# SwiGLU feed-forward: the early loads in one queue, and the first tokens in two pieces

## The chip, the cores and the metric

The kernel runs on one core of a Trainium2 chip. The metric is the device time of one execution in microseconds. All positions below are microseconds from the start of the profiled span. TensorE is written PE, VectorE DVE, ScalarE ACT, GpSimd POOL and SyncE SP; SPq and ACTq are the rows of the DMA issues of SP and ACT, and PEld the weight loads of PE.

## The reference

```python
B, S, D, F = 1, 2048, 512, 1376      # bf16: x (B, S, D), w_gate, w_up (D, F), w_down (F, D)

def reference(x, w_gate, w_up, w_down):
    g = silu(x @ w_gate)
    u = x @ w_up
    return (g * u) @ w_down
```

## The kernel before

The 2048 tokens are four chunks of 512. F is cut into ten whole tiles of 128 and a rest of 96. For each chunk and tile, PE makes a gate product (kind G) and an up product (kind U) of 128 F rows by 512 tokens in one PSUM bank each: four steps over D (`dk`), each of two matmuls of 64 columns that stand side by side in the array. ACT puts Silu of G into `sg_sb`, DVE multiplies it with U into `hT_sb`. The rest of 96 is handled by the kinds X and Y. At the end PE multiplies `hT_sb` with `w_down` (kind O), ACT and DVE copy the banks to `o_sb`, and SP (once ACT) stores them.

The products need the tokens transposed, D on the partitions, in `xT_sb`. For chunks 1 to 3 and for tokens 256 to 511 a transposing DMA does this (`load_x`; the load of tokens 256 to 511 is called `x0b`). Tokens 0 to 255 come in by a plain load into `xn_sb` (name `xn`), with two neighbouring tokens on each partition: partition p holds tokens 2p and 2p + 1. PE transposes them with an identity, in four groups of kind T: for piece i = 0, 1 and half h = 0, 1 of D, four transposes into a bank. DVE copies the half 0 to `xT_sb` and ACT the half 1 (`xt_ready[i, h]`). Since the columns of `xT_sb` are then every second token, the first two stores write every second row (`rows_of`).

The order on each engine is written out by hand:

- ACT first issues the load of the gates of F tiles 0 and 1 (`wg0`, `loads_on_scalar`), then does a dummy Silu that brings in its table, then its work in the order of the groups.
- SP issues `xn`, then the ups of F tiles 0 and 1 (`wu0`), then `x0b`, then the slabs of F tiles 2 to 3, 4 to 6 and 7 to 10 (gates, ups), the last ups, `x1` to `x3`, and the parts of `w_down`. All are issued without a wait. The stores come behind.
- POOL makes the index tile from which DVE makes the identity.
- PE runs `N_WARM` = 6 matmuls of ones, 512 columns wide, and `N_FILL` = 2 of 128 columns, into a bank that is not yet used. Then it waits for the identity and for `xn`, and runs the 16 transposes. Then the products of F tiles 0 and 1 of chunk 0 in parts: G of tile 0 for tokens 0 to 127 and 128 to 255, then G of tile 1, U of tile 0, U of tile 1 for tokens 0 to 255, then the same four for tokens 256 to 511. From there each product is whole. `need(name)` is a wait of PE for a load, made once for each load; `after` is a wait for a copy or another step of ACT or DVE.

A load's semaphore is named after it (`s_xn`, `s_wg0`, `s_wu0`, `s_x0b`). PE counts its finished groups in `s_P`.

Of the kernel before, what the change touches and what calls it, by code (L numbers as in the profile page):

```python
# [6 lines left out]
BF16 = mybir.dt.bfloat16  # L7
FP32 = mybir.dt.float32

N_WARM = 6  # L10
N_FILL = 2


def bass_standalone__swiglu_ffn__prompt_kernel(nc, x, w_gate, w_up, w_down, out):
    _, S, D = x.shape
    F = w_gate.shape[1]
    P = 128
# [12 lines left out]
    HT = SC // 2  # L30
    HC = P // 2
    NXN = HT // P
# [5 lines left out]
    xf = x[0]  # L38
    of = out[0]
# [7 lines left out]
    with ExitStack() as es:  # L47
# [20 lines left out]
        xn_sb = sb("xn_sb", [P, NXN, D], BF16)  # L68
# [12 lines left out]
        def load_sem(name):  # L81
            loads[name] = sem(f"s_{name}")
            return loads[name]
# [6 lines left out]
        def load_x(eng, name, t0, t1):  # L90
            eng.dma_start_transpose(
                xT_sb[:, :, t0:t1], xf[t0:t1, :]
            ).then_inc(load_sem(name), 16)

        def load_w(eng, name, src, base, f0, f1):
            eng.dma_start(
                w_sb[:, :, base + f0:base + f1],
                src[:, f0:f1].rearrange("(k p) f -> p k f", p=P),
            ).then_inc(load_sem(name), 16)

        slabs = [(0, 2), (2, 4), (4, 7), (7, NFT)]
        slab_of = {ft: a for a, b in slabs for ft in range(a, b)}

        def load_slab(eng, a, b):
            load_w(eng, f"wg{a}", w_gate, 0, a * P, min(b * P, F))
            load_w(eng, f"wu{a}", w_up, UPH, a * P, min(b * P, F - 32))

        def loads_on_scalar(act):
            load_w(act, "wg0", w_gate, 0, 0, slabs[0][1] * P)

        def loads_on_sync(sp):
            sp.dma_start(
                xn_sb[:, :, :].rearrange("p j d -> p (j d)"), xf[0:HT, :].rearrange("(p j) d -> p (j d)", j=NXN)
            ).then_inc(load_sem("xn"), 16)
            load_w(sp, "wu0", w_up, UPH, 0, slabs[0][1] * P)
            load_x(sp, "x0b", HT, SC)
            for a, b in slabs[1:]:
                load_slab(sp, a, b)
            load_w(sp, "wut", w_up, F - (F - 32), F - 32, F)
            for c in range(1, NSC):  # L120
                load_x(sp, f"x{c}", c * SC, (c + 1) * SC)
            sp.dma_start(
                wd_sb[:, 0:NFF, :], w_down[0:NFF * P, :].rearrange("(k p) d -> p k d", p=P)
            ).then_inc(load_sem("wd"), 16)
            for c in range(NSC):
                sp.dma_start(
                    wdt_sb[R * c:R * (c + 1), :, :], w_down[NFF * P:F, :].rearrange("(q p) d -> p q d", p=R)
                ).then_inc(load_sem(f"wdt{c}"), 16)
            sp.dma_start(wdl_sb[:, :], w_down[NFF * P:F, LASTA:D]).then_inc(load_sem("wdl"), 16)
# [7 lines left out]
        def add_group(kind, **what):  # L137
            g = dict(kind=kind, at=len(groups), bank=banks[len(groups) % NB], readers=[], **what)
            groups.append(g)
            return g  # L140
# [9 lines left out]
        def tview(bank):  # L150
            return bank[:, 0:P].bitcast(BF16).rearrange("p (k t) -> p k t", k=2)
# [60 lines left out]
        for i in range(NXN):  # L212
            for h, eng in enumerate("DA"):
                g = add_group("T", i=i, h=h)
                op = add_op(
                    eng, g, kind="copy", out=xT_sb[:, 2 * h:2 * h + 2, i * P:(i + 1) * P],
# [15 lines left out]
        for at in range(NST):  # L232
            j, c = divmod(at, NSC)
            t = c * TPC + j
            ob = at % NOS
            end = at == NST - 1
            for c0, c1 in [(0, LASTA), (LASTA, LASTB), (LASTB, D)] if end else [(0, D)]:
                g = add_group("O", t=t, c0=c0, c1=c1, c=c)
# [3 lines left out]
                    eng, g, kind="copy", out=o_sb[ob][:, c0:c1], src=g["bank"][:, 0:c1 - c0],  # L242
# [4 lines left out]
            n_store[ob] += 2 if end else 1  # L247

        def rows_of(t):
            if t < NXN:  # L250
                return of[0:HT, :].rearrange("(p j) d -> j p d", j=NXN)[t]
            return of[t * P:(t + 1) * P, :]

        def on_sync(sp):
            loads_on_sync(sp)
            for t, c0, c1, ob, eng, n in stores:
                if (c0, c1) == (0, LASTA):
                    continue
                sp.wait_ge(s_A if eng == "A" else s_D, n)
                sp.dma_start(rows_of(t)[:, c0:c1], o_sb[ob][:, c0:c1]).then_inc(s_out[ob], 16)  # L260
            for i in range(NST, NST + NOS):
                sp.wait_ge(s_out[i % NOS], 16 * n_store[i % NOS])
# [4 lines left out]
            ).then_inc(s_I, 1)  # L267

        def on_scalar(act):
            loads_on_scalar(act)  # L270
            act.activation(adummy[:, 0:4], zero_c, ACT.Silu)
            for op in act_ops:
                act.wait_ge(s_P, op["g"]["at"] + 1)
                if op["kind"] == "silu":
                    if op["free"]:
                        act.wait_ge(s_D, op["free"])
                    fn = ACT.Silu
                else:
                    if op["stored"][1]:
                        act.wait_ge(*op["stored"])  # L280
                    fn = ACT.Copy
                act.activation(op["out"], op["src"], fn).then_inc(s_A, 1)  # L282
            for t, c0, c1, ob, eng, n in stores:
                if (c0, c1) == (0, LASTA):
                    act.wait_ge(s_A, n)
                    act.dma_start(rows_of(t)[:, c0:c1], o_sb[ob][:, c0:c1]).then_inc(s_out[ob], 16)
# [16 lines left out]
        def on_tensor(pe):  # L303
            landed = set()

            def need(name):
                if name not in landed:
                    pe.wait_ge(loads[name], 16)
                    landed.add(name)
# [34 lines left out]
            def warm(n, width):  # L344
                for i in range(n):
                    pe.matmul(banks[NB - 1][:, 0:width], lhsT=ones_w, rhs=ones_m[:, 0:width], start=True, stop=True)  # L346

            warm(N_WARM, SC)
            warm(N_FILL, P)
            pe.wait_ge(s_J, 1)  # L350
            need("xn")
            for g in groups[:NT]:
                for k in range(2):
                    dk = 2 * g["h"] + k
                    for m in (0, HC):
                        ins = pe.transpose(  # L356
                            tview(g["bank"])[m:m + HC, k, :], xn_sb[:, g["i"], dk * P + m:dk * P + m + HC], ident[:, :],
                        )
                ins.then_inc(s_P, 1)
# [126 lines left out]
        on_sync(nc.sync)  # L486
        on_gpsimd(nc.gpsimd)
        on_scalar(nc.scalar)
        on_tensor(nc.tensor)
        on_vector(nc.vector)  # L490

# [27 lines left out]
```

## Time and profile before

| | us |
|---|---|
| median of 3 runs | 120.34 (120.11 to 120.6) |
| the profiled execution | 120.53 |
| its span, from the first to the last instruction | 119.2 |

| engine | busy us | share of the span | instructions |
|---|---|---|---|
| PE | 116.3 | 98% | 1341 |
| PEld | 61.7 | 52% | 1342 |
| DVE | 43.5 | 36% | 68 |
| ACT | 35.5 | 30% | 61 |

| part of the DMA rate (40 slices of the span, 2.98 us each) | GB/s |
|---|---|
| slices 1 to 4 | 88, 303, 344, 363 |
| slices 5 to 9 | 166, 210, 221, 323, 199 |

PE is busy for nearly the whole span, but that share says nothing of its rate: a matmul's duration is from its start to its modelled end, and durations overlap. The rate is read from the distance of starts, or from the length of a stretch and the number of matmuls in it. The kernel's loads are all in by the tenth slice; the stores come in the last quarter. In the timeline, a row stands for a run of like instructions: start, length, engine, line, operation, tiles, count, and in brackets the idle time before it with what ended it.

### The profile page before, as it was taken

How to read it: one execution, taken by the hardware profiler on the slowest of the kernel's cores; microseconds unless marked ns; L12 is line 12 of the kernel's file. 1: busy time of each engine (PE TensorE's matmuls, PEld its weight loads, DVE VectorE, ACT ScalarE, POOL GpSimd, SP SyncE). 2: the span in 40 equal slices, each digit the busy share in tenths (PEclk: the TensorE clock that was granted, in tenths of full speed). 3: DMA queues.
4: the chain of work that ended last, by engine and by line, in shares of the span. 5: the costliest groups of instructions: out<-in, count | busy, mean ns of one | idle time of the engine just before them, and what ended most of it. 6: DMA issues, size and time to landing. Idle time of an engine off the chain costs nothing.

```text
span 119.2 us, 2983 instructions
## 1 busy us (share of the span) xinstructions
PE 116.3 (98%) x1341; PEld 61.7 (52%) x1342; DVE 43.5 (36%) x68; ACT 35.5 (30%) x61; POOL 0.4 (0%) x5
## 2 busy tenths in 40 slices
PE   7999999999999999999999999999999999999993
PEld 2795555555555555555555555544444444464452
DVE  0115434444334444344353344369800040214331
ACT  4223343262442363432454423470000030213001
POOL 1000000000000000000000000000000000000000
DMA  3999999980000000000000000000000023050612
GB/s 88 303 344 363 166 210 221 323 199 23 0 5 0 0 0 5 0 0 5 0 5 0 0 0 0 5 0 0 5 0 5 0 87 95 0 176 22 203 44 88
DMA packets 16508, 8.92 MB, mean 75 GB/s; under 512 B 8560, under 2 KB 16368, under 8 KB 16496
## 3 DMA queue, kind: packets, MB, share of 16 engines
q1 hardware_dynamic: 15824, 8.38, 27.5%
q10 hardware_dynamic: 672, 0.36, 1.0%
q8 instruction: 10, 0.16, 0.6%
q14 instruction: 2, 0.02, 0.0%
HBM read 4.81 MB, written 2.10 MB: 58 GB/s over the span
## 4 chain that ended last, share of the span: by engine, by line
PE 98%; issue 0%; DVE 0%
PE bank L336 59%; PE bank L429 24%; PE bank L406 7%; PE bank L382 3%; PE bank L346 2%; PE bank L393 1%; PE bank L356 1%; DVE o_sb L300 0%; PE bank L481 0%
## 5 line engine op out<-in xcount | busy, mean ns | idle before, releaser
L336 PE MATMUL bank<-xT_sb,w_sb 128*64 128x512 bf16 (+2 forms) x680 | 70.5, 370 | 0.0
L336 PEld LDWEIGHTS bank<-xT_sb,w_sb 128*64 128x64 bf16 x680 | 38.5, 112 | 31.1
L296 DVE TENSOR_TENSOR hT_sb<-sg_sb,bank 128x512 bf16<-128x512 f32 x40 | 27.5, 687 | 40.9 <-PE bank L336 36.6
L282 ACT ACTIVATE sg_sb<-bank 128x512 f32<-128x512 f32 x40 | 23.8, 596 | 41.2 <-PE bank L336 41.1
L429 PE MATMUL bank<-wd_sb,hT_sb 32*128 32x512 bf16 x480 | 26.9, 374 | 0.0
L429 PEld LDWEIGHTS bank<-wd_sb,hT_sb 32*128 32x128 bf16 x480 | 12.7, 93 | 13.3 <-issue 0.4
L300 DVE CAST o_sb<-bank 128x512 bf16<-128x512 f32 (+1 forms) x11 | 6.4, 604 | 25.2 <-PE bank L429 19.9
L282 ACT ACTIVATE o_sb<-bank 128x512 bf16<-128x512 f32 (+1 forms) x7 | 3.7, 580 | 32.9 <-PE bank L429 25.9
L406 PE MATMUL bank<-wd_sb,hT_sb 128*128 128x512 bf16 (+2 forms) x59 | 8.7, 307 | 0.2 <-issue 0.2
L406 PEld LDWEIGHTS bank<-wd_sb,hT_sb 128*128 128x128 bf16 x60 | 4.6, 97 | 4.6 <-issue 0.4
L296 DVE TENSOR_TENSOR ht_sb<-sgy_sb,yu_sb 32x512 bf16<-32x512 f32 x8 | 5.5, 683 | 0.4
L382 PE MATMUL bank<-xT_sb,w_sb 128*64 128x512 bf16 x32 | 4.1, 379 | 0.0
L296 DVE TENSOR_TENSOR ht_sb<-sgx_sb,bank 32x512 bf16<-32x512 f32 x4 | 2.8, 691 | 3.5 <-ACT sgx_sb L282 3.5
L282 ACT ACTIVATE sgx_sb<-bank 32x512 f32<-32x512 f32 x4 | 2.3, 587 | 4.5 <-PE bank L382 4.5
L346 PE MATMUL bank<-const-bfloat16-1.0 128*128 128x512 bf16 (+1 forms) x8 | 2.9, 545 | 0.8 <-PEq L504 0.8
L429 PE MATMUL bank<-wdt_sb,ht_sb 32*128 32x512 bf16 (+1 forms) x48 | 3.3, 371 | 0.0
L382 PEld LDWEIGHTS bank<-xT_sb,w_sb 128*64 128x64 bf16 x32 | 1.8, 110 | 1.6
L282 ACT ACTIVATE sgy_sb<-bank 64x512 f32<-64x512 f32 x4 | 2.4, 589 | 0.1
L346 PEld LDWEIGHTS bank<-const-bfloat16-1.0 128*128 128x128 bf16 x8 | 1.0, 137 | 2.4 <-issue 2.4
L429 PEld LDWEIGHTS bank<-wdt_sb,ht_sb 32*128 32x128 bf16 x48 | 1.3, 93 | 1.3
L393 PE MATMUL bank<-xT_sb,w_sb 128*64 128x512 bf16 x16 | 1.9, 379 | 0.0
L300 DVE COPY xT_sb<-bank 128x256 bf16<-128x256 bf16 x2 | 0.6, 292 | 3.1 <-PE bank L356 2.9
(17 smaller groups left out, 8.2 us busy)
## 6 DMA issues: line engine op xcount, KB each, us to landing
out_dram<-o_sb SPq DMA_DIRECT2D x15, 128.0 KB, 1.8
wd_sb<-in_w_down_dram SPq DMA_DIRECT2D x1, 1280.0 KB, 9.1
w_sb<-in_w_up_dram SPq DMA_DIRECT2D x2, 256.0 KB, 4.2
w_sb<-in_w_gate_dram SPq DMA_DIRECT2D x1, 480.0 KB, 5.8
w_sb<-in_w_up_dram SPq DMA_DIRECT2D x1, 448.0 KB, 7.8
w_sb<-in_w_gate_dram SPq DMA_DIRECT2D x1, 384.0 KB, 4.5
w_sb<-in_w_up_dram SPq DMA_DIRECT2D x1, 384.0 KB, 4.9
wdt_sb<-in_w_down_dram SPq DMA_DIRECT2D x4, 96.0 KB, 7.6
```

Of the source, the lines that this page charges most:

```text
L282: act.activation(op["out"], op["src"], fn).then_inc(s_A, 1)
L296: ins = dve.tensor_tensor(op["out"], op["a"], op["b"], ALU.mult)
L300: ins = dve.tensor_copy(op["out"], op["src"])
L336: ins = pe.matmul(g["bank"][m:m + HC, n0:n1], lhsT=w_sb[:, dk, col + m:col + m + HC], rhs=xT_sb[:, dk, c * SC + n0:c * SC + n1], start=(dk ...
L346: pe.matmul(banks[NB - 1][:, 0:width], lhsT=ones_w, rhs=ones_m[:, 0:width], start=True, stop=True)
L356: ins = pe.transpose(tview(g["bank"])[m:m + HC, k, :], xn_sb[:, g["i"], dk * P + m:dk * P + m + HC], ident[:, :],)
L382: ins = pe.matmul(g["bank"][m:m + HC, :], lhsT=w_sb[:, dk, XC0 + m:XC0 + m + HC], rhs=xT_sb[:, dk, c * SC:(c + 1) * SC], start=(dk == 0), ...
L393: ins = pe.matmul(g["bank"][y0:y1, :], lhsT=w_sb[:, dk, YC0:YC0 + 64], rhs=xT_sb[:, dk, c * SC:(c + 1) * SC], start=(dk == 0), stop=(dk == ...
L406: ins = pe.matmul(g["bank"][:, 0:c1 - c0], lhsT=hT_sb[:, fk, t * P:(t + 1) * P], rhs=wd_sb[:, fk, c0:c1], start=(start and fk == 0), stop= ...
L429: ins = pe.matmul(g["bank"][:, 0:c1 - c0], lhsT=h(r, g["t"]), rhs=w[R * r:R * (r + 1), c0:c1], start=(start and n == 0), stop=final, tile_ ...
```

## The change

SP issues all early loads, in this order: tokens 0 to 127 (`xn0`), tokens 128 to 255 (`xn1`), `wg0`, `wu0`, `x0b`, and the others as before. ACT issues none of them. Each piece of tokens has 1 KB on a partition, where the one load had 2 KB. PE runs five wide warm-ups instead of six, waits for `xn0` ahead of the transposes of piece 0, runs `N_GAP` = 2 more matmuls of ones with 128 columns behind them, waits for `xn1`, and transposes piece 1. Its products follow in the same order as before. The first two stores write rows in a row.

```diff
-N_WARM = 6
+N_WARM = 5
 N_FILL = 2
+N_GAP = 2
...
-        def loads_on_scalar(act):
-            load_w(act, "wg0", w_gate, 0, 0, slabs[0][1] * P)
-
         def loads_on_sync(sp):
-            sp.dma_start(
-                xn_sb[:, :, :].rearrange("p j d -> p (j d)"), xf[0:HT, :].rearrange("(p j) d -> p (j d)", j=NXN)
-            ).then_inc(load_sem("xn"), 16)
+            for i in range(NXN):
+                sp.dma_start(xn_sb[:, i, :], xf[i * P:(i + 1) * P, :]).then_inc(load_sem(f"xn{i}"), 16)
+            load_w(sp, "wg0", w_gate, 0, 0, slabs[0][1] * P)
             load_w(sp, "wu0", w_up, UPH, 0, slabs[0][1] * P)
             load_x(sp, "x0b", HT, SC)
...
         def rows_of(t):
-            if t < NXN:
-                return of[0:HT, :].rearrange("(p j) d -> j p d", j=NXN)[t]
             return of[t * P:(t + 1) * P, :]
...
         def on_scalar(act):
-            loads_on_scalar(act)
             act.activation(adummy[:, 0:4], zero_c, ACT.Silu)
...
             pe.wait_ge(s_J, 1)
-            need("xn")
             for g in groups[:NT]:
+                if g["i"] and not g["h"]:
+                    warm(N_GAP, P)
+                need(f"xn{g['i']}")
                 for k in range(2):
                     dk = 2 * g["h"] + k
```

## The prediction

> **What bounds the kernel now.** I read the chain that ended last first, then the two rates of TensorE (PE), then the SyncE queue (SPq) and the DMA rate by stretches. The chain's early pieces, as start, length and what:
>
> ```profile
> 0.73 0.04 issue
> 0.77 2.93 PE bank L346 x8
> 3.71 0.09 issue
> 3.80 1.06 PE bank L356 x16
> 4.87 18.07 PE bank L336 x200
> ```
>
> Warm-up matmuls (L346) run until the tokens land, 16 transposes (L356) follow, then L336, the gate and up products. They start at 4.70 in the timeline, and behind that the chain has no break but 0.16 us at 108.5. So the change acts on the time before the products, or by opening a hole behind their start.
>
> TensorE has two rates. One shape in two stretches, 4.7 to 5.9 and 6.4 to 8.6 (count, busy, mean ns, idle):
>
> ```profile
> L336 PE MATMUL bank<-xT_sb,w_sb 128*64 128x256 bf16 x4 | 0.6, 421 | 0.0
> ...
> L336 PE MATMUL bank<-xT_sb,w_sb 128*64 128x256 bf16 x44 | 2.6, 274 | 0.0
> ```
>
> The granted clock reads 1.00 in both, so the step has to be read from durations. The warm-ups' weight loads stand 0.427 us apart for 512 columns; in the long stretches 160 matmuls of 512 columns take 17.27 us, two side by side, so 0.216 us for each pair. That is half. The weight loads of line 336, by the tile view 177 ns at most and 110 in the median, average 165 from 5.2 to 5.9 and 110 from 6.4 on; between them, at about 6.2, I put the step. Call the products' start G (4.70) and the step S (6.2). Work done between G and S counts half, so the end lies at a constant plus (G + S)/2, and **a shift of the end is half the sum of the shifts of G and S**. All prices below use this.
>
> The early loads, from SPq's timeline and from the DMA issues (KB, us from issue to landing):
>
> ```profile
> 0.74 0.40 SPq L112 DMA_DIRECT2D xn_sb<-in_x_dram  x1
> 1.20 0.41 SPq L96 DMA_DIRECT2D w_sb<-in_w_up_dram  x1
> 1.66 1.30 SPq L91 DMA_TRANSPOSE xT_sb<-in_x_dram  x1
> 3.02 0.57 SPq L96 DMA_DIRECT2D w_sb<-in_w_gate_dram  x1
> ```
> ```profile
> w_sb<-in_w_gate_dram ACTq DMA_DIRECT2D x1, 256.0 KB, 3.7
> xn_sb<-in_x_dram SPq DMA_DIRECT2D x1, 256.0 KB, 2.9
> ```
>
> So xn lands at 0.74 + 2.9 = 3.64 and the first transpose starts 0.16 later; wg0 (ScalarE's queue, issued at 0.74 too) lands at 4.4. By the timeline the first VectorE copy ends at 4.55, 0.15 before the product that needs it. wg0 and that copy are nearly level in front of G.
>
> **The change part by part.**
>
> *One warm-up less.* 0.43 us goes. The eight occupy TensorE's input until 0.77 + 6 x 0.427 + 2 x 0.107 = about 3.5; now until 3.1. It stood in front of a wait for xn, so it gains nothing unless the first piece lands before 3.5.
>
> *Tokens in two pieces.* The DMA rates of the stretches 1.5-2, 2-2.5, 2.5-3, 3-3.5, 3.5-4, 4-4.4, 4.4-5 and 5-5.5 are 90, 164, 274, 286, 345, 345, 287 and 259 GB/s, so the bytes moved by 2.5, 3.0, 3.5, 4.0, 4.4, 5.0 and 5.5 are about 127, 264, 407, 580, 718, 890 and 1,019 thousand. xn's 262 thousand are through at 3.0 and it lands at 3.64: a lag of 0.64. The last of the four early loads makes 1,049 thousand, reached at 5.6, and the transposing load lands at 1.66 + 4.7 = 6.36: a lag of 0.76. If the engines take one queue's loads in order at these rates, piece 0 (131 thousand, 2.5) lands at 3.15 and piece 1 at 3.64. Piece 0's eight transposes then start at 3.31 and take half of the present 0.85, until 3.73; the two gap matmuls (2 x 0.107) reach to 3.95. Piece 1's transposes run from 3.95 to 4.37; today they end at 4.65. The new wait on piece 1 holds the eight transposes and all products queued behind it, and VectorE's and ScalarE's second copies; by this sum it has passed 0.3 us before TensorE gets there. Bounds for piece 1: issue 1.20 plus 2.9 is 4.1 at worst, 0.15 too late.
>
> *wg0 behind two pieces on SPq.* The first SPq issues start 0.46 apart (0.74, 1.20, 1.66), so wg0 is issued at 1.66 instead of 0.74. Its cover is the DMA engines' backlog: 524 thousand bytes are through at 3.84, and with the lag it lands at 4.48. If it were bound by its issue, the nearest row, the same size without much ahead of it, is xn's 2.9: 4.56. Its own 3.7 includes its wait behind xn; it gives 5.36. I take 4.48, and 4.4 (as now) and 5.36 as ends. The first product, 0.15 behind, starts at 4.63. The copies are no longer late: piece 0's first copy, which today starts 0.46 after the first transpose, starts near 3.8 and ends at 4.1. What is late next is wg0 alone: G moves from 4.70 to 4.63, or to 4.55 and 5.5 at the ends.
>
> *Everything behind, 0.92 later in issue.* Two issues are put ahead of wu0, one of them new and one moved from ScalarE's queue, so each later load is issued 2 x 0.46 us later. wu0 at worst lands at 1.20 + 0.92 + 4.1 = 6.22; its first use is near 6.3 (behind two 128-wide steps and one 256-wide step of eight matmuls, 1.7 us at the slow rate from 4.70, less the step). The transposing load at worst lands at 7.28; the second halves that need it start about 7.1, from the first Silu at 7.85 less its four pairs of 0.108 (half of 0.216) and the last one's 0.27. That is 0.2 us lost at most; at the rates above both land as today, at 5.3 and 6.4, and I cost them at nothing. The next gate slab, issued at 3.02 and landing 4.1 later, is due when the second halves end (7.1 + 16 x 0.108 = 8.8): 1.7 us of slack against 0.92. Later slabs and the token loads, with products of 17 us a chunk ahead of them, have more.
>
> *ScalarE without its issue:* its table load starts up to 0.46 earlier, and its next work is at 4.47. Nothing. *Rows of the first two stores:* contiguous instead of every second row, both long before the last stores. Nothing.
>
> **Sum.** G moves by -0.07, S by nothing: -0.035. The profiled execution took 120.53 for a span of 119.2, so 1.33 lie around it; 119.2 - 0.04 + 1.33 = 120.49. That execution is 0.19 above the median of 120.34, so a median of 120.3. With the ends of wg0 and S held, -0.08 to +0.4: 120.26 to 120.74. About 0.5%, 0.6 us, is what a measurement of this kernel can tell from no change; that takes 1.2 us in G + S together.
>
> [...]
>
> **The rivals.**
>
> *Slower: wg0 is bound by its issue, and the clock step follows the products.* It lands at 5.36, G is 5.5 (+0.8). [...] For it: 0.92 us later in one queue, and a hole ahead of G that the warm-ups no longer fill. Against it: the byte count, which has the engines busy from 2.0 on (shares of 0.93 and more).
>
> *Faster: the step comes earlier.* The three times of this one program span 0.49 us, which by the rule of halves is 1 us in S, so S may not be fixed to the program. In the new kernel TensorE's early work is closer together (the break before the transposes shrinks). S before 5.0 gives over 0.5%; with no slow products left at all (S = G = 4.63) the end moves by (0.07 + 1.57)/2 = 0.8: 119.5. Against it: no row shows the step at another place. [...]
>
> *The change doesn't overlap:* both pieces land together near 3.64 because the second is at the first one's heels. Then transposes run from 3.80 through 4.85 with the gap matmuls' 0.21 added, G is near 4.9, +0.1: 120.4. For it: piece 1's worst landing, 4.1. Against it: the byte count, which is 0.5 us apart for the two.
>
> **How the numbers follow.** Forecast (120.3, its own range 120.0 to 120.7) 0.32 and no overlap (120.4) 0.15: together 0.47 within 0.5%. Slower by over 0.5% 0.33, because wg0's later issue, a longer hole and a later step all pull one way. Faster by over 0.5% 0.20, since only the step can do it: G alone yields at most 0.08. The range reaches from the fast rival's end, 119.5, to just past the slow rival's, 121.3, where a step a little later still would end; beyond it about 0.1 is left.
>
> **What would show it.** Right: transposes in two groups of eight with two 128-wide warm-ups between them, the first near 3.3; the first product at 4.55 to 4.7; the weight loads' fall to 110 ns near 6.2; wg0's landing 2.8 us after its issue at 1.66; no idle of TensorE behind the first product. Wrong: wg0 landing after 5.1, a pause at the second halves near 7 (transposing load late), or the fall to 110 ns anywhere but within 1 us of 6.2.

## The result and the profile after

The changed kernel takes 120.32 us in the median of 22 runs (120.11 to 120.65). The kernel before, run beside it on the same chip, takes 120.07 in 22 runs (119.72 to 120.6). The ratio is 1.0022, with a 95% interval of 1.0012 to 1.0033. The change costs 0.25 us. It costs most at the fast end: the shortest time rose by 0.39 us, the lower and upper quartiles by 0.22 and 0.18, the longest by 0.05. Ratios in this document leave out executions more than 1.5% above the fastest of their kernel, one of e3 and one of e5.

The profiled execution of the changed kernel took 120.21 us for a span of 118.9. Its chain that ended last begins in another way (start, length, what):

```profile
0.74 0.39 SPq L111
...
1.65 3.30 DMA w_sb<-in_w_gate_dram
4.95 0.04 issue
5.00 17.61 PE bank L331 x200
```

The warm-ups and transposes are gone from it. In their place stand SyncE's first issues and wg0's 3.30 us from issue to landing. The first product starts at 5.00 instead of 4.70. The waits up to 9 us name the loads, where the same profile of the kernel before has no wait of TensorE for a load (who waited for what: us in total, times, longest; PEld and PE show the same wait twice):

```profile
PEld bank L331 <- DMA w_sb<-in_w_gate_dram: 0.6, 1, 0.6
PE bank L331 <- DMA w_sb<-in_w_gate_dram: 0.5, 1, 0.5
...
PEld bank L331 <- DMA xT_sb<-in_x_dram: 0.2, 1, 0.2
```

The second load named is x0b. SyncE's timeline has the issues near where the prediction put them (1.66, 2.12 and 2.58):

```profile
1.65 0.43 SPq L97 DMA_DIRECT2D w_sb<-in_w_gate_dram  x1
2.12 0.51 SPq L97 DMA_DIRECT2D w_sb<-in_w_up_dram  x1
2.67 1.30 SPq L92 DMA_TRANSPOSE xT_sb<-in_x_dram  x1
```

x0b lands 4.1 us behind its issue, at 6.82 instead of 6.35; wu0 at 5.78 instead of 5.30. TensorE's timeline has the transposes in two groups:

```profile
3.21 0.64 PE L353 MATMUL bank<-ident,xn_sb 128*64 128x128 bf16 x8
3.77 0.39 PE L341 MATMUL bank<-const-bfloat16-1.0 128*128 128x128 bf16 x2
4.10 0.41 PE L353 MATMUL bank<-ident,xn_sb 128*64 128x128 bf16 x8
```

So the pieces do overlap: the tokens are transposed by 4.5, and the copies that the first product needs, those of piece 0, end at 4.27. The second group took 0.41 us where the first took 0.64: the step to the faster rate lies between them, some 2 us earlier than in the profile before. That is why this span is shorter than the profiled one of before although the kernel is slower. The products confirm it; from 5.0 to 6.5 they run at the duration that the kernel before had only from 6.4 on (274 ns, and 421 from 4.7 to 5.9):

```profile
L331 PE MATMUL bank<-xT_sb,w_sb 128*64 128x256 bf16 x20 | 1.3, 272 | 0.0
```

Two profiles that differ in the step's place can't be set against each other by their spans. More profiles of both kernels are needed, and they come below.

### The profile page after: what moved, and what is told of

Same layout as the page of the kernel before. It is cut to its first block, busy times and chain, and to the rows that moved or that the text cites. A ratio compares the mean times of both kernels' runs of the same rounds, so it can differ in the third digit from the quotient of the medians.

```text
span 118.9 us, 2986 instructions
## 1 busy us (share of the span) xinstructions
PE 115.6 (97%) x1342; PEld 60.8 (51%) x1343; DVE 43.5 (37%) x68; ACT 35.5 (30%) x61; POOL 0.4 (0%) x5
## 3 DMA queue, kind: packets, MB, share of 16 engines
HBM read 4.81 MB, written 2.10 MB: 58 GB/s over the span
## 4 chain that ended last, share of the span: by engine, by line
PE 94%; DMA 3%; SPq 1%; issue 0%; DVE 0%
PE bank L331 58%; PE bank L426 24%; PE bank L403 7%; PE bank L379 3%; DMA w_sb<-in_w_gate_dram 3%; PE bank L390 1%; SPq L111 1%; DVE o_sb L295 0%; PE bank L478 0%
## 5 line engine op out<-in xcount | busy, mean ns | idle before, releaser
L331 PEld LDWEIGHTS bank<-xT_sb,w_sb 128*64 128x64 bf16 x680 | 37.8, 110 | 31.8 <-DMA w_sb<-in_w_gate_dram 0.6
L379 PEld LDWEIGHTS bank<-xT_sb,w_sb 128*64 128x64 bf16 x32 | 1.8, 110 | 1.6
```

Of the source, the lines that this page charges most:

```text
L331: ins = pe.matmul(g["bank"][m:m + HC, n0:n1], lhsT=w_sb[:, dk, col + m:col + m + HC], rhs=xT_sb[:, dk, c * SC + n0:c * SC + n1], start=(dk ...
L379: ins = pe.matmul(g["bank"][m:m + HC, :], lhsT=w_sb[:, dk, XC0 + m:XC0 + m + HC], rhs=xT_sb[:, dk, c * SC:(c + 1) * SC], start=(dk == 0), ...
```

## The experiments

The theories. **A**: loads land late because SyncE issues them later. Rivals: **B**, the smaller pieces or the single queue slow the engines whatever the issue time; **C**, fewer warm-ups or the gap move the step. Later ones: **F**, the loss sits with wu0 and x0b in executions whose step is early, against **G**, wg0 alone.

**e4: TensorE's part undone.** In the changed kernel:

```diff
-N_WARM = 5
+N_WARM = 6
-N_GAP = 2
+N_GAP = 0
```

> The changed kernel with TensorE's warm-ups of before: six wide ones, none in the gap between the pieces. Theory A: wg0 alone sets the first product, near 5.0, and the ratio stays at 1.0015 to 1.003. Rival C (the clock step follows the warm-ups): the ratio comes back to 1.000. In all four runs, if the clock step does not depend on the program, the place where the weight loads fall to 110 ns differs between the profiles, by more than the first product's start does.

Measured: 1.0020 (1.0003 to 1.0036), the first product at 4.94; wg0, wu0 and x0b land at 4.90, 5.96 and 6.98. Its waits:

```profile
PEld bank L331 <- DMA w_sb<-in_w_gate_dram: 0.8, 1, 0.8
...
PEld bank L331 <- DMA w_sb<-in_w_up_dram: 0.3, 1, 0.3
PEld bank L331 <- DMA xT_sb<-in_x_dram: 0.2, 1, 0.2
```

The ratio stays where the changed kernel's is, and TensorE waits for the same loads. Within that interval the warm-ups are not the cause, and C falls for this change.

**e1: wg0 back on ScalarE's queue**, the pieces as in the changed kernel:

```diff
-            load_w(sp, "wg0", w_gate, 0, 0, slabs[0][1] * P)
...
         def on_scalar(act):
+            load_w(act, "wg0", w_gate, 0, 0, slabs[0][1] * P)
```

> The changed kernel with wg0 issued by ScalarE at 0.74 again; the token pieces stay on SyncE. Theory A (wg0 is late because it is issued 0.9 us later): wg0 lands near 4.4 to 4.5, the first product starts near 4.55 to 4.65, the time comes back to that of the kernel before or just under it, a ratio of 0.998 to 1.000. Rival B (the smaller packets of the two pieces, or the pieces' order, hold up the DMA engines): wg0 still lands near 4.9 and the ratio stays at 1.002. Rival C (one wide warm-up less and the gap move the clock step): the ratio stays at 1.002 too, with wg0 early.

Measured: 1.0014 (0.9994 to 1.0035), which the time alone can't tell from the kernel before or from the changed one. In the profile wg0 lands at 4.01, earlier than in any other, so B's small pieces don't hold it up. But piece 1, issued at 1.20 as in the changed kernel, now lands at 4.34 instead of 3.30: ScalarE's load, issued 0.46 before it, has gone ahead of it. TensorE's timeline:

```profile
4.38 0.64 PE L353 MATMUL bank<-ident,xn_sb 128*64 128x128 bf16 x8 [0.21 <-DMA xn_sb<-in_x_dram]
4.81 1.54 PE L331 MATMUL bank<-xT_sb,w_sb 128*64 128x128 bf16 x20
```

The wait has moved from wg0 to piece 1, and the first product to 4.81. A had wg0 back early, though not this early (4.4 to 4.5), and its first product (4.55 to 4.65) was wrong.

**e2: only wg0 moved to SyncE**, behind the single token load, in the kernel before:

```diff
+            load_w(sp, "wg0", w_gate, 0, 0, slabs[0][1] * P)
             load_w(sp, "wu0", w_up, UPH, 0, slabs[0][1] * P)
...
-            loads_on_scalar(act)
```

> The kernel before with one edit: wg0 is issued by SyncE right behind the single token load, so at 1.20 instead of 0.74, and wu0 and x0b 0.46 later. Theory A: wg0 lands 3.3 us after its issue (as in the changed kernel), 4.5, if the engines run dry behind the tokens, the first product near 4.65 to 4.75, ratio 1.000 to 1.001. Rival B2 (one queue instead of two is what slows wg0, whatever its issue time): it lands near 4.9, the first product near 5.0, ratio 1.002.

Measured: 1.0006 (0.9987 to 1.0026); wg0, issued at 1.19, lands at 4.32 and the first product starts at 4.59. One queue is not slower here than two for wg0 (4.40 in the kernel before), so B's second form falls too.

**e3: wg0 issued at 1.66 on ScalarE's own queue**, in the kernel before:

```diff
         def loads_on_scalar(act):
+            for i in range(2):
+                act.dma_start(wdl_sb[:, 64 * i:64 * (i + 1)], ...)
             load_w(act, "wg0", w_gate, 0, 0, slabs[0][1] * P)
```

> The kernel before with one edit: ScalarE issues two small loads (the last columns of w_down, 12 KB each) ahead of wg0, so that wg0 is issued near 1.66, still on its own queue; all of SyncE's early issues stay where they are. Theory A: wg0 lands near 4.9 to 5.0, the first product near 5.0, ratio 1.0015 to 1.003. Rival B2 (queues, not issue times): it lands at 4.4 to 4.5, ratio 1.000.

Measured: 1.0108 (1.0079 to 1.0138). The chain:

```profile
1.66 4.78 DMA w_sb<-in_w_gate_dram
6.43 0.04 issue
6.48 17.51 PE bank L339 x200
```

wg0 lands at 6.44, not at 5.0; wu0, issued 0.46 before it, lands at 4.48, 0.8 earlier than in the kernel before. The two loads have exchanged places. A's direction held and its size was far off: here an issue 0.9 later loses 2.0, as another queue's load is now in front.

**e6: one more small load ahead of wg0**, in the changed kernel; there are two profiles of it:

```diff
+            sp.dma_start(wdl_sb[:, :], w_down[NFF * P:F, LASTA:D]).then_inc(load_sem("wdl"), 16)
             load_w(sp, "wg0", w_gate, 0, 0, slabs[0][1] * P)
```

> The changed kernel with one small load (24 KB, the last columns of w_down) put ahead of wg0 on SyncE: wg0, wu0 and x0b are issued 0.46 later, with 5% more bytes ahead. Theory A: wg0 is issued at 2.12 and lands near 5.4, the first product near 5.45, x0b near 7.3; ratio to the kernel before 1.005 to 1.008. If bytes and not issue times decide: wg0 lands less than 0.1 us later than in the changed kernel, 5.0, ratio 1.002 to 1.003.

> The kernel with the small load ahead of wg0 once more. Its first look had wg0 at 4.98 as in the changed kernel, but was the fastest of its four times. Theory A, issue times decide: in this look wg0 lands later than that, near 5.4, or wu0 and x0b land 0.5 later than the changed kernel's. If bytes decide: all three as in the changed kernel.

Measured: 1.0141 (1.0092 to 1.0191, from four times). wg0, issued at 2.12, lands at 4.98 in the first profile and 5.08 in the second. Beside the 4.95 above that is almost no delay, as bytes would have it, and A's 5.4 is wrong. But 4.95 is the latest of three: beside the 4.57 and 4.59 of the changed kernel's other profiles below, it is 0.4 to 0.5 later, as much as its issue. So this run does not decide between bytes and issue times for wg0. wu0 and x0b land at 6.35 and 7.42, then 6.02 and 7.08, so these came 0.2 to 0.6 later, as A has it. The loss of 1.5 us in the median is more than any landing explains; of it more below.

**e7: the second and third issue exchanged** (piece 0, wg0, piece 1):

```diff
-            for i in range(NXN):
-                sp.dma_start(xn_sb[:, i, :], ...)
+            load_piece(sp, 0)
             load_w(sp, "wg0", w_gate, 0, 0, slabs[0][1] * P)
+            load_piece(sp, 1)
```

> The changed kernel with SyncE's second and third issue exchanged: piece 0, wg0, piece 1. Theory A, the third issue lands late whatever it carries: wg0 lands near 4.3, piece 1, issued at 1.66 behind it, at 4.4 to 4.9; its transposes end near 5.0 and the first product starts near 5.0; ratio 1.001 to 1.003. Rival E, the load of wg0 itself is slow (its 512-byte rows): wg0 still needs 3.3 us or more from its issue, piece 1 lands by 4.1, the first product at 4.6, ratio 0.999 to 1.001.

Measured: 1.0073 (1.0040 to 1.0105). wg0 needs 2.9 us and lands at 4.10, piece 1 at 4.44, the first product starts at 4.91, all near what A has; E falls. The ratio is larger than A said. wu0 and x0b land late too, at 6.50 and 7.53, but in this profile TensorE waits for neither: its step stands at 6.7, and with the first product at 4.91 the rule of halves (and the 113.9 us that the table below gives for the rest) makes a span of 119.7, as measured.

**e5: piece 1 on ScalarE's queue**, in the changed kernel:

```diff
-            for i in range(NXN):
-                sp.dma_start(xn_sb[:, i, :], ...)
+            load_piece(sp, 0)
...
         def on_scalar(act):
+            load_piece(act, 1)
```

> The changed kernel with piece 1 issued by ScalarE at 0.74, so that SyncE issues piece 0 at 0.74, wg0 at 1.20, wu0 at 1.66, x0b near 2.2. Theory A (a load lands late because it is issued late): wg0 lands 3.1 us after its issue, as where it was issued at 1.20 behind the single load, so near 4.3; piece 1 lands by 3.6; the first product starts near 4.45, 0.5 before the changed kernel's and 0.2 before the kernel's before. Ratio 0.997 to 1.000. Rival D (two queues at once hold each other up, as piece 1 was held up behind wg0 when that was on ScalarE's queue): piece 0, piece 1 or wg0 lands 0.4 us later than that, the first product at 4.8 or later, ratio 1.001 or more.

Measured: 1.0037 (1.0013 to 1.0061). wg0 lands at 4.29 as A has it, but piece 0 at 3.39 instead of 2.89, as D has it. The transposes then set the first product, at 4.84:

```profile
3.52 0.64 PE L356 MATMUL bank<-ident,xn_sb 128*64 128x128 bf16 x8 [0.24 <-DMA xn_sb<-in_x_dram]
4.09 0.39 PE L344 MATMUL bank<-const-bfloat16-1.0 128*128 128x128 bf16 x2
4.42 0.58 PE L356 MATMUL bank<-ident,xn_sb 128*64 128x128 bf16 x8
```

**More profiles of both kernels and of e2**, since the profiles differ in the step's place.

> The kernel before once more, one look. If landings repeat: wg0 4.3 to 4.5, wu0 near 5.3, x0b near 6.4, the first product at 4.6 to 4.7. The clock step, if it follows nothing in the program, stands somewhere else than at 6.2. In any case the span should be 113.8 plus the first product's start, plus half of what the step lies behind it, plus waits for wu0 and x0b.

> The kernel before a third time, for the spread of its landings: wg0 4.3 to 4.5, wu0 near 5.3, x0b near 6.4, the first product at 4.6 to 4.7, the clock step anywhere.

> The changed kernel once more, one look. Theory A: wg0 lands at 4.8 to 5.1, wu0 at 5.7 to 6.0, x0b at 6.7 to 7.0, the first product near 5.0. If the late wg0 of the first look was an accident of that execution: wg0 by 4.6 and the first product by 4.7.

> The changed kernel a third time, for where wg0, wu0 and x0b land: so far 4.96 and 4.60, 5.79 and 5.88, 6.82 and 6.91. If x0b is what always comes late and wg0 only at times: x0b at 6.8 to 7.0 again, wg0 anywhere from 4.6 to 5.0. The span is 113.8 plus the first product's start (with half the step's distance), or 113.8 + 5.1 where the step is early, as x0b then sets the end.

> The kernel before with wg0 on SyncE behind the tokens, once more. Its first look had x0b at 7.13, which with an early step would give 120.5, but seven of its twelve times lie below 120.2. So x0b should land earlier in this look, at 6.4 to 6.8; if it lands at 7.1 with an early step and a time below 120.2, x0b's landing does not set the fast end, and theory F falls.

The landings, the first product's start G, the last weight load of 165 ns or more as the step S, and the span:

| profile | wg0 | wu0 | x0b | G | S | span |
|---|---|---|---|---|---|---|
| before, 1 | 4.40 | 5.30 | 6.35 | 4.70 | 6.0 | 119.2 |
| before, 2 | 4.36 | 5.19 | 6.24 | 4.65 | 5.5 | 118.9 |
| before, 3 | 4.34 | 5.18 | 6.22 | 4.64 | 4.0 | 118.5 |
| changed, 1 | 4.95 | 5.78 | 6.82 | 5.00 | 3.4 | 118.9 |
| changed, 2 | 4.59 | 5.88 | 6.91 | 4.64 | 6.4 | 119.4 |
| changed, 3 | 4.57 | 5.77 | 6.80 | 4.62 | 5.0 | 118.9 |
| e2, 1 | 4.32 | 6.08 | 7.12 | 4.59 | 5.9 | 119.2 |
| e2, 2 | 4.28 | 5.95 | 6.99 | 4.54 | 4.3 | 119.1 |

The step stands anywhere between 4.0 and 6.0 in the kernel before and between 3.4 and 6.4 in the changed one. wg0 is late by 0.6 in one profile of the changed kernel in three; in the others it is 0.2 later and G is as before. wu0 and x0b are late in all three, by 0.5 to 0.7. Where the step is early, the changed kernel's span is 118.9 against 118.5, and where it is late the two are alike: the second profile of the changed kernel is 0.2 above the first of before, with a step 0.4 later, which is worth 0.2.

The rule of halves tells what each profile lost, with 113.9 us for the rest of the span as the three of before give it. Changed 1: 113.9 + 5.00 is its 118.9, so the late first product is all. Changed 2: its G and S give its span, and TensorE waits for no load. Changed 3: G and S give 118.7, and the 0.2 above it is as long as its only wait behind G, the 0.2 us for x0b.

**e8: wu0 and x0b alone issued 0.92 later**, in the kernel before; wg0 stays on ScalarE's queue at 0.74:

```diff
+            for i in range(2):
+                sp.dma_start(wdl_sb[:, 64 * i:64 * (i + 1)], ...)
             load_w(sp, "wu0", w_up, UPH, 0, slabs[0][1] * P)
```

> The kernel before with one edit: SyncE issues two small loads (12 KB each, the last columns of w_down) between the tokens and wu0, so that wu0 and x0b are issued 0.92 later, as in the changed kernel, and wg0 stays at 0.74 on ScalarE's queue. Theory F (the loss sits with wu0 and x0b, in executions whose clock step is early): the first product stays at 4.6 to 4.7, x0b lands near 6.9, the fastest times go up by 0.4 to 0.5 us and the slowest stay, ratio 1.001 to 1.003. Theory G (the loss is wg0's landing alone): x0b may land late, and the ratio stays within 0.999 to 1.001.

Measured: 1.0034 (1.0019 to 1.0049), times of 120.16 to 120.69 beside 119.68 to 120.61 of the kernel before. The waits of its profile, whose step came before the first product:

```profile
PEld bank L339 <- DMA w_sb<-in_w_up_dram: 0.3, 1, 0.3
PEld bank L339 <- DMA w_sb<-in_w_gate_dram: 0.3, 1, 0.3
PEld bank L339 <- DMA xT_sb<-in_x_dram: 0.2, 1, 0.2
```

With wu0 at 5.82, x0b at 6.86 and the first product at 4.72, 0.02 to 0.08 behind the three profiles before, the loss of the changed kernel is there: the shortest time up by 0.48, the longest by 0.08. wg0's issue was left alone, but the tokens and wg0 landed some 0.15 later in this profile, which F had not expected, and the two small loads put 24 KB more ahead of wu0; the first product follows little. So G falls as the only cause. F fits the fast end; it doesn't account for the upper quartile, which rose by 0.53.

**e9: all early loads issued early, without the gap.** e5 with `N_WARM = 6` and `N_GAP = 0`, which the landings of e5 pointed to as a version that might beat both:

> The changed kernel with piece 1 on ScalarE's queue, as in e5, and with six wide warm-ups and no matmuls in the gap. In e5 wg0, wu0 and x0b landed at 4.29, 5.15 and 6.13, all a little before the kernel before's, and only the transposes were late: they took from 3.52 to 4.74, with the gap. Theory F: without the gap the transposes end near 4.3, the first product starts near 4.45, 0.2 before the kernel before's, and no load stops TensorE: ratio 0.998 to 0.9995. If the warm-ups or the gap are not what made e5 slow, or its landings do not repeat: ratio 1.002 or more, as e5's 1.0037.

Measured: 1.0012 (0.9991 to 1.0032): no gain is shown. G is 4.58, but wu0 and x0b land at 5.96 and 6.96 instead of e5's 5.14 and 6.12, and TensorE's weight loads wait 0.4 and 0.2 us for them. They are issued at 1.66 and 2.20, 0.5 later than in the kernel before; e5 issued them at the same times, so issue time alone doesn't set the landing. No version run here is shown to beat the kernel before.

## Why the prediction was wrong

**The direction was wrong; the size stayed inside the 0.5%.** Forecast was a shift of -0.035 us; measured is a ratio of 1.0022. That the median of 120.32 lies at the forecast 120.3 is luck: the forecast was made from 120.34, and the kernel before came out at 120.07 beside it.

**The step that failed: "I cost them at nothing".** wu0 and x0b, issued 0.92 later, were to land as today "at the rates above", those of the kernel before. They land 0.5 to 0.7 later, because the rates did not stay. First the kernel before, then the changed one (stretch, length, busy time by engine, granted clock, DMA share, GB/s):

```profile
3.00:3.50 0.50, 0.50 (x4) 0.16 (x2) 0.00 (x0) 0.00 (x0) 0.00 (x0) 1.00 0.93 286
```
```profile
3.00:3.50 0.50, 0.50 (x9) 0.30 (x9) 0.00 (x0) 0.00 (x0) 0.00 (x0) 1.00 0.57 100
```

In the other two profiles of each kernel the rate here is 321 and 335 before, and 160 and 152 after. With wg0 issued at 1.65, some 275 thousand bytes had moved by 3.0, by the rates of its windows, and 262 of these are the tokens': little of wg0 was yet moving, and I take it that the backlog had run short. This stretch alone overstates the loss, since those two profiles of the kernel before have 135 and 122 GB/s from 2.5 to 3.0. Summed from the start, the changed kernel is 77 thousand bytes behind at 3.5 and 174 thousand at 6.0, in the mean of three profiles each. So more than half is lost later, where the engines are not idle. Again before, then changed:

```profile
5.00:5.50 0.50, 0.50 (x15) 0.47 (x14) 0.00 (x0) 0.28 (x1) 0.00 (x0) 1.00 1.19 259
```
```profile
5.00:5.50 0.50, 0.50 (x18) 0.50 (x20) 0.00 (x0) 0.00 (x0) 0.00 (x0) 1.00 1.19 208
```

The share is the same 1.19 (it sums the packets' times, and they overlap), and a fifth fewer bytes move. Why is not shown. e2 lacks the early hole (342 and 338 GB/s from 3.0 to 3.5), falls to 56 and 89 from 5.0 to 5.5, and has wu0 and x0b as late as the changed kernel; so the early hole is not the whole cause.

The way of counting was right. In all 17 profiles x0b lands 0.7 to 0.8 us after the bytes of the four early loads (with any small load put ahead) have moved, and the prediction's lag was 0.76. It put their last byte at 5.6, by the rates before; in the changed kernel it comes at 6.1 to 6.2. The bound that the prediction gave for x0b by its issue, 7.28, was too late, and the byte count, 6.36, too early; it lands at 6.8 to 6.9.

**What is late next.** The prediction named wg0 alone. With wg0 at 4.57 and 4.59 in two profiles, its 4.48 was near, and the first profile's 4.95 lay between the ends given. In those two the first product starts at 4.62 and 4.64, the forecast 4.63, but that is no gain: the kernel before has 4.64 and 4.65 in its other profiles, and the 4.70 of the prediction was its latest. In the third it starts 0.3 later. Two smaller terms were off. The product starts 0.04 behind wg0's landing, not 0.15, which was its distance from a copy. And the second group of transposes, put at 3.95 to 4.37, starts at 4.10 and reaches to 4.7 where the step is late, so in changed 2 and 3 it leaves TensorE no idle time before G. e8 shows the rest of the loss with wg0's issue left alone.

**The clearance of x0b was counted at the slow rate.** The second halves were put near 7.1, from a profile with the step at 6.2. With an early step, the first halves' 16 pairs at the faster rate bring TensorE there at G + 16 x 0.108, about 6.4, where x0b in the kernel before has just landed (6.2 to 6.4) and in the changed one has not. So this part of the loss falls on executions with an early step, which fits the shortest and longest times; the quartiles, both up by about 0.2, are between. That early steps occur could be read from nothing but the spread of the three times, and the prediction used that only for a rival.

**What held.** The rule of halves: the three spans of the kernel before, less G and half of S - G, give 113.9, 113.8 and 113.9 (in the third profile S is before G and counts nothing), and the second of the changed kernel 113.9. The overlap of the pieces: transposes at 3.21 and 4.10, two groups of eight, so the rival without overlap falls. The issue times to 0.1 us. The rows of the stores and ScalarE's earlier start show in no wait.

**The rivals.** The slow one named a later issue in one queue, but for wg0 alone, and its end of 121.3 is 1.0 above the measured 120.32: wg0 at 5.36 was never seen in the changed kernel. The later step that this end, and the 5.1 set for wg0's landing, count on was the author's estimate, and no run shows it: in the changed kernel's three profiles the step stands at 3.4, 6.4 and 5.0 with the first product at 5.00, 4.64 and 4.62, and so doesn't follow the products. The fast one, a step at another place, is real, but it is no effect of the change: the kernel before has it too (4.0 to 6.0).

**What stays open.** Why wg0 lands 0.4 us later in some executions with the same issue times. Why the DMA rate is lower from 5 to 6. Why e5's times are slower than its one profile explains, when e9's are not shown to be. Why e6 and e7 lose 1.5 and 0.9 us: steps at 6.7 (e7) and 9.0 (e6's second profile) explain those two spans by the rule of halves, and both have TensorE idle before its products, but whether such a hole makes the step late was not tested; in the changed kernel's first profile the step had come before the hole. And e2: its x0b lands at 7.0 and 7.1, late as in the changed kernel, and its second profile took 120.42 by it, yet seven of its twelve times lie below 120.2, and its ratio of 1.0006 shows no loss. Those executions must have had earlier landings than both profiles, or F is not the whole of it.

## What to carry to other kernels

Here a later issue was covered only as long as the backlog lasted: from 3.0 to 3.5 the rate was 286 GB/s or more before and 160 or less in the changed kernel. So take the moment at which the engines would run out of issued work, and don't carry the rates of one order of issue over to another. In this kernel the rates fell a second time with the engines busy (208 GB/s for 259 from 5.0 to 5.5, at the same share of 1.19), which no count of the backlog would have shown. Moving one issue from a second queue to the first, and splitting another, put off the issue of all behind them by 0.9 to 1.0 us, and wu0 and x0b landed 0.5 to 0.7 later. The load that pays can be the one with the least clearance in the fastest execution, not in the profiled one: here x0b, at 6.8 to 6.9 where an early step brings TensorE to it at about 6.4. If times of one program spread by more than the effect that is sought, look at several profiles before reading a difference from two.

## What was not expected of the hardware

- The place where TensorE goes over to its faster rate (weight loads of 110 ns, and of 165 to 177 before it) varies from 3.4 to 6.4 us between three executions of the changed kernel, worth up to 0.9 us at the end by the rule of halves, (6.4 - 4.64)/2. Once, in e6's second profile, it was at 9.0, and the span was 120.9. From 5.2 to 8.8 its weight loads average 174 ns:

```profile
L331 PEld LDWEIGHTS bank<-xT_sb,w_sb 128*64 128x64 bf16 x46 | 3.4, 174 | 1.0 <-DMA w_sb<-in_w_gate_dram 0.6
```

  What sets the place is not shown, nor why it was so late there; TensorE was idle for 0.4 us ahead of its products in that profile, and for 0.5 in the changed kernel's first, which had the step at 3.4.
- Two 128-column matmuls between two groups of transposes take more than their 0.21 us (half of the 0.427 of a 512-column warm-up): the first group starts at 3.21 and the second at 4.10, 0.89 apart, where eight transposes need 0.43 at the slow rate (half of the 0.85 of 16 in the kernel before). Why is not shown. The transposes do run at the faster rate, 0.41 us for eight against 0.64.
- The early loads land here in the order of their issue over both queues. In all 17 profiles, of the loads issued before 3.5 us none lands ahead of one that was issued more than 0.01 us earlier on either queue. So what was issued ahead on the other queue moves a landing at the same issue time: piece 1 lands at 3.30 without wg0 ahead of it and at 4.34 with it (e1), and wg0, issued at 1.66, lands at 4.95 or earlier behind the two pieces and at 6.44 behind the tokens and wu0 (e3).
